# Thresholded attention and a SoLU feed-forward block on one core: the first four units' product with v taken in place, in 32-row tiles

## The chip, the core and the metric

The kernel runs on one core of a Trainium2 chip. The metric is the device time of one execution in microseconds (us). A core has a matrix engine (PE; its weight loads are listed apart as PEld), a vector engine (DVE), a scalar engine (ACT), a GpSimd engine (POOL), a queue engine that only issues transfers (SyncE, SP), and 16 DMA engines that all queues share. Each engine works through its own instructions in order and waits on semaphores where it needs another's result.

## The reference, cut to what matters

```python
# q, k, v: (8 batches, 8 heads, 576 positions, 64), float32; tau = 0.02
scores = (q @ k.T) / sqrt(64)
thresh = max(scores, axis=-1) - tau
scores = where(scores >= thresh, scores, -1e9)
attn = exp(scores - max(scores)); attn = attn / (sum(attn) + 1e-9)
x = attn @ v                          # then (batch, position, head * 64): 4608 x 512
h = x @ w_in                          # 512 -> 1024; the weights arrive as 64-bit floats
solu = h * softmax(h)
ln = (solu - mean) / sqrt(var + 1e-6) * g_ln
out = ln @ w_out                      # 1024 -> 512
```

## The kernel before

**Units and slots.** Heads go in pairs; a pair's two heads lie in the two 64-row halves of the tiles. A batch has four pairs. Its first 512 positions are cut into two kinds of 256 queries, its last 64 positions are kind 2. A unit is (batch, kind, pair); it has two slots r = 0 and 1 of 128 queries and two heads each. A batch has 18 slots, the program 144, one a round; some 17 rounds follow in which only the feed-forward block is left.

**One round** (the loop in the last 200 lines) writes each engine's instructions of that round, in an order set by hand (`tc.manual_schedule`): PE multiplies the slot's scores (`scores`, L480) into two PSUM tiles; DVE takes the row maxima (`maxes`, L502); ACT clips (`ramp`, L517) and takes the exponentials (`exps`, L526); a round later POOL normalises (`normalise`, L533 to L536) and DVE turns the weights in 32 x 32 blocks (`blocks`, L548) into the unit's tile T. PSUM has two tiles for the scores and two pairs of banks, `p0` and `p1`, for all else: the product with v takes one (`take("pv")`), a feed-forward tile's h one until it is multiplied, its output one.

**The product with v.** A block turn leaves each 32-key block of a query group on that group's own 32 partitions, so the keys do not lie where v has them. With slot r = 1, `blocks` therefore issues three transfers on SyncE's queue (L557 once, 576 KB; L559 twice, 288 KB each) that carry T into `wT`, where keys lie on 64 partitions as v's rows do. Some rounds later (`pv_due`) `attend_steps` multiplies: nine key chunks, two row halves, two heads, 36 products in tiles of 64 rows and 64 columns with 128 queries as the moving side (L590), each product two pairs of weight load and matmul. `attended` copies the result to xh on ACT (L622). The first four units, (0, 0, pair 0 to 3), are multiplied in rounds 5, 7, 9 and 10.

**The feed-forward block.** When a kind's four units are done, two tiles of 128 tokens are ready. A tile takes four quarter steps on PE, one a round: h in two halves (L655), and, after softmax, statistics, the exchange of halves by DMA (`ff_swap`, L737) and a block turn (`ff_turn`, L747), the product with w_out in two halves (L760). The first tile's h is multiplied in rounds 11 and 12. A line `if rnd == 13` lets the second tile's h follow before the first tile's product with w_out.

**The start.** Rounds 0 to 15 also decode one piece of the weights each (`weight_load` on SyncE's queue, L275; L286, L292, L306 and L309 on DVE; L291 on ACT; L319 on POOL). Pair 1, 2 and 3 of batch 0 are turned by PE in rounds 0, 2 and 4 with both bank pairs in use (`whole_pair`, L345). v is loaded by half batches: half 0 in rounds 0 and 1, half 1 in rounds 3 and 5 (L177, L182). Its columns hold four of each partition's positions; columns 4 to 7 hold those of the partition 64 away.

Of the kernel before, what the change touches and what calls it, by code (L numbers as in the profile page):

```python
# [8 lines left out]
F32 = mybir.dt.float32  # L9
# [7 lines left out]
P = 128  # L17
# [3 lines left out]
def kernel(  # L21
# [27 lines left out]
    nc = tc.nc  # L49
    B, H, S, D = q.shape  # L50
# [39 lines left out]
    NK = S // 64  # L90

    halves = {}
# [3 lines left out]
    units = {}  # L96
    xh = {}
# [3 lines left out]
    pairs_free = ["p0", "p1"]  # L101

    def take(name):
        tag = pairs_free.pop(0)
        return tag, ps_mm.tile([P, 1024], F32, tag=tag, name=name)
# [44 lines left out]
    def load_v(b, hf, parts=(0, 1, 2)):  # L150
        d = halves.setdefault((b, hf), {})
        hs = slice(4 * hf, 4 * hf + 4)

        if b > 1:
            if 0 in parts:
                d["v"] = loads.tile([P, 4, NK, D], F32, tag="v", bufs=3, name="v")
            to = d["v"].rearrange("p h m d -> p h (m d)")
            rows = v_rows[64 * (H * b + 4 * hf) :][0:256]
            for part in parts:
                nc.sync.dma_start(**(  # L160
                    dict(
                        out=to.rearrange("p (e o) n -> p o e n", o=2)[:, 0],
                        in_=rows.rearrange("(e r) n -> r e n", e=2),
                    ),
                    dict(out=to[:, 1], in_=rows[64:192]),
                    dict(out=to[ROWS[1], 3], in_=rows[0:64]),
                    dict(out=to[ROWS[0], 3], in_=rows[192:256]),
                )[part])
            return
        if 0 in parts:  # L170
            d["v"] = loads.tile([P, 4, NK, D], F32, tag="v", bufs=3, name="v")
        rest = v[b, hs, 0:SM, :].rearrange("h (p t) d -> p h (t d)", t=4)
        for part, to, rows, of in (
            (0, 0, slice(0, P), slice(0, P)), (1, 4, ROWS[0], ROWS[1]), (1, 4, ROWS[1], ROWS[0])
        ):
            if part in parts:
                nc.sync.dma_start(  # L177
                    out=d["v"][rows, :, to : to + 4].rearrange("p h t d -> p h (t d)"),
                    in_=rest[of],
                )  # L180
        for rows in ROWS if 2 in parts else ():
            nc.sync.dma_start(  # L182
                out=d["v"][rows, :, NK - 1], in_=v[b, hs, SM:S, :].rearrange("h p d -> p h d")
            )

    qk_rows = {
        nm: x.rearrange("b h (i a t) d -> a (b h i) (t d)", a=2, t=NK)
# [167 lines left out]
    def source(i):  # L355
        b, hp = divmod(i, NP)
        return halves[b, hp // 2], 2 * (hp % 2)
# [182 lines left out]
    def blocks(s):  # L540
        b, kind, hp, r = slots[s]
        key = (b, kind, hp)
        if r == 0:
            units[key] = dict(T=work.tile([P, NB, 2, 2, 32], F32, tag="T", name="T"))
        u = units[key]
        T = u["T"]
        for h, w in enumerate(live.pop(s)["w"]):
            nc.vector.transpose(out=T[:, :, r, h, :], in_=w)  # L548
        if r == 0:
            return  # L550


        T = T.rearrange("p (c m) r h x -> p c (m r h x)", c=2)
        u["wT"] = wT = work.tile([P, 2, NK, 2, 2, 32], F32, tag="wT", bufs=2, name="wT")
        to = wT.rearrange("p g m r h x -> p g (m r h x)")
        if kind < 2:
            nc.sync.dma_start(out=to[:, 1], in_=T[32:96])  # L557
            for half in range(2):
                nc.sync.dma_start(out=to[ROWS[half], 0], in_=T[96 * half : 96 * half + 32])  # L559
            return  # L560
        for g in range(2):
            for half in range(2):
                of = 64 * half + 32 * g
                nc.sync.dma_start(out=to[ROWS[half], g], in_=T[of : of + 32])  # L564

    def attend_steps(key):
        b, kind, hp = key
# [97 lines left out]
    def ff_max(t):  # L667
        d = ffn[t]
        d["nm"] = small.tile([P, 1], F32, tag="hm", name="hm")
        nc.vector.tensor_reduce(out=d["nm"], in_=d["h"], axis=AX.X, op=ALU.max, negate=True)  # L670

    def ff_exp(t):
        d = ffn[t]

        starts.append(t)
        tag = "xh1" if rnd > NS and len(starts) % 2 else "u"
        d["u"] = work.tile([P, DFF], F32, tag=tag, bufs=1, name="u")
        d["se"] = small.tile([P, 1], F32, tag="se", name="se")
        nc.scalar.activation(  # L679
            out=d["u"], in_=d["h"], func=AF.Exp, bias=d["nm"], scale=1.0, accum_out=d["se"]  # L680
        )

    def ff_mul(t):
        d = ffn[t]
        nc.vector.tensor_tensor(out=d["u"], in0=d["h"], in1=d["u"], op=ALU.mult)  # L685
        pairs_free.append(d["tag"])

    def ff_sum(t):
        se = ffn[t]["se"]
        nc.gpsimd.tensor_scalar(out=se, in0=se, scalar1=1e-9, scalar2=None, op0=ALU.add)  # L690
        nc.gpsimd.tensor_tensor(out=se, in0=se, in1=mone[:, 0:1], op=ALU.pow)
# [110 lines left out]
    PER = NS // B  # L802
    LAG_PV = 3

    pv_due = []
    for s, (b, kind, hp, r) in enumerate(slots):
        if r == 1:
            pv_due.append((s + LAG_PV + (s < 6 or s in (11, PER - 1, PER + 9)), (b, kind, hp)))

    def first_slot(i):  # L810
        return PER * (i // NP) + 2 * (i % NP)
# [12 lines left out]
    load_at = {}  # L824
# [12 lines left out]
    for i in range(2 * NP, NPAIR, 2):  # L837
        b, hf = divmod(i // 2, 2)
# [3 lines left out]
        for nm, pieces_at in zip("qk", ats):  # L842
            for a, at in enumerate(pieces_at):
                at += PER * b
                if b == 2:
                    of = at - 3 - (at in (PER + 7, PER + 9))
                else:
                    of = (at - 3) // 4 * 4
# [19 lines left out]
    with tc.manual_schedule():  # L868
# [14 lines left out]

        pieces = {r: x for x, r in enumerate(range(16))}
        whole = {0: 1, 2: 2, 4: 3}
        for r, hf, parts in ((0, 0, (0,)), (1, 0, (1, 2)), (3, 1, (0,)), (5, 1, (1, 2))):
            load_at[r] = [lambda hf=hf, parts=parts: load_v(0, hf, parts)]

        ready = []
        rnd = 0  # L890
# [7 lines left out]
        while True:  # L898
# [10 lines left out]
            if rnd == NS:  # L909
# [6 lines left out]
                    cur = None  # L916
                    quarter = 0
                assert quarter != 3
            if rnd == 13:
                prev, cur, quarter = cur, None, 0  # L920
            if (
                cur is None and quarter == 0 and ready and ready[0][0] <= rnd
# [9 lines left out]
            if more:  # L932
# [3 lines left out]
                while preps and preps[0][0] <= rnd and preps[0][1] <= room:  # L936
                    _, n, make, _ = preps.pop(0)
# [27 lines left out]
                weight_c(pieces[rnd - 1])  # L965
            for job in middle.pop(rnd, []):
                job()
            due = bool(pv_due) and pv_due[0][0] <= rnd
            step = None
            if quarter < 2 and cur is not None:  # L970
# [17 lines left out]
            if step == ("h", 0):  # L988
                ff_h(cur, 0, rnd + 1 < NS, beside)
                quarter = 1  # L990
            elif step == ("h", 1):
                ff_h(cur, 1, None, beside)
                quarter = 2
                by = rnd + 2 * (rnd == 14)
                late.setdefault(by, []).append(lambda t=cur: (ff_max(t), ff_exp(t)))
                late.setdefault(by + 1, []).append(lambda t=cur: (ff_mul(t), ff_sum(t)))
                middle.setdefault(by + 2, []).append(lambda t=cur: ff_stats(t))
                if rnd + 6 < NS:
                    norms[by + 3] = cur
                else:  # L1000
                    late.setdefault(rnd + 2, []).append(lambda t=cur: ff_norm(t))
                middle.setdefault(by + 3, []).append(lambda t=cur: (ff_norm2(t), ff_swap(t)))

                at = by + 4 if more or not ready or len(ready[0][1][0]) == 1 else rnd + 6
                if cur == (0, 1, 1):
                    middle.setdefault(rnd + 6, []).append(lambda t=cur, at=rnd + 6: ff_turn(t, at))
                else:
                    late.setdefault(at, []).append(lambda t=cur, at=at: ff_turn(t, at))
                if not more:
                    between.append(cur)  # L1010
                    cur = None
                    quarter = 0
            elif step == ("o", 0):
                if prev is not None:
                    ff_o(prev, 0)
                quarter = 3
            elif step == ("o", 1):
                if prev is not None:
                    ff_o(prev, 1)
                    last = not (more or ready or cur or between)  # L1020
                    begin.setdefault(rnd + 1, []).append(lambda t=prev, last=last: ff_out(t, last))
                    late.setdefault(rnd + 1, []).append(lambda t=prev, last=last: ff_store(t, last))
                prev, cur = cur, None
                quarter = 0
            if attending is not None:
# [3 lines left out]
                b, kind, hp = attending  # L1029
# [16 lines left out]
            if rnd in pieces:  # L1046
                x = pieces[rnd]
# [45 lines left out]
```

## Time and profile before

| | |
|---|---|
| time, three runs | 861.92, 864.92, 865.21 us; median 864.92 |
| profiled execution | 869.02 us, its span 867.2 us |
| busy share of the span | PE 95%, weight loads 70%, DVE 79%, ACT 66%, POOL 58% |
| mean granted PE clock | 0.976 |
| DMA | 168.54 MB, mean 194 GB/s; data queue q1 76.3% of the 16 engines |
| chain that ended last | PE 79%, DMA 8%, DVE 4%, ACT 4% |

The page gives one profiled execution: busy times by engine, the span in 40 slices of 21.7 us (a digit is a busy share in tenths), the DMA queues, the chain of work that ended last followed back from the end, and the groups of instructions that cost most. A row of the timeline gives start, duration, engine, line, operation, output and input, and in brackets the idle time before it and what ended it. A busy PE is not one at its peak, since matmuls overlap.

### The profile page before, as it was taken

The page shows a single profiled execution, that of the slowest core. Times are in us where ns is not written, and L with a number is a line of the kernel's source. Part 1 is how long each engine was busy: PE and PEld are TensorE (multiplying, and loading weights), DVE is VectorE, ACT ScalarE, POOL GpSimd, SP SyncE. Part 2 cuts the span into 40 slices and gives each one's busy share as a digit, 9 for nine tenths or more (in the row PEclk, how much of TensorE's full clock was granted, in tenths as well). Part 3 has the DMA queues.
Part 4 walks back from the last instruction along what each step waited for, and adds up shares of the span by engine and source line. Part 5 has one row for each costly group of instructions (what it writes and reads, how often), then busy time and mean ns, then how long its engine had stood idle before and what let it go on. Part 6 is the DMA issues. An engine that isn't in the chain of part 4 may idle for free.

```text
span 867.2 us, 36122 instructions
## 1 busy us (share of the span) xinstructions
PE 822.9 (95%) x15361; PEld 605.8 (70%) x15361; DVE 681.7 (79%) x1248; ACT 573.6 (66%) x1153; POOL 500.2 (58%) x938
## 2 busy tenths in 40 slices
PE   5668799989999999999999999999999999999997
PEld 3446466667677776899777766777777777777655
DVE  4988878878788888888888887888788887787361
ACT  5877876667677767777666766777677776776121
POOL 2886656556756666565656665565666655555120
PEclk9769999999999999999999999999999999999999
DMA  8999887998888878898888787888788787655312
GB/s 256 252 251 227 191 210 181 210 236 210 215 206 226 208 183 214 208 221 203 196 207 225 207 187 185 217 220 207 183 230 229 197 192 180 163 136 139 69 38 62
DMA packets 83712, 168.54 MB, mean 194 GB/s; under 512 B 15448, under 2 KB 45152, under 8 KB 83552
## 3 DMA queue, kind: packets, MB, share of 16 engines
q1 hardware_dynamic: 82416, 164.25, 76.3%
q8 instruction: 120, 1.97, 1.0%
q10 hardware_dynamic: 1136, 2.00, 0.7%
q14 instruction: 40, 0.33, 0.1%
HBM read 46.14 MB, written 9.44 MB: 64 GB/s over the span
## 4 chain that ended last, share of the span: by engine, by line
PE 79%; DMA 8%; DVE 4%; ACT 4%; SPq 2%; issue 2%; POOL 1%; ACTq 0%; DVEq 0%
PE o_ps L760 26%; PE h_ps L655 20%; PE pv L590 14%; PE s_ps L480 14%; DMA wT<-T 6%; PE h_ps L645 3%; ACT w L517 1%; DVE w L502 1%; ACT w L526 1%; DVE T L548 1%; DMA q<-in_q_dram 1%; DMA qT<-flip 1%; SPq L564 1%; DMA k<-in_k_dram 1%; SPq L559 0%
## 5 line engine op out<-in xcount | busy, mean ns | idle before, releaser
L760 PE MATMUL o_ps<-w,uT 64*64 64x256 f32 x4608 | 271.6, 378 | 1.2 <-ACT xe L622 0.6
L502 DVE CUSTOM_DVE_ANT_0 w<-s_ps,tau_t 128x576 f32<-128x576 f32 x280 | 200.0, 751 | 90.0 <-PE s_ps L480 61.6
L517 ACT ACTIVATE w<-s_ps,nth 128x576 f32<-128x576 f32 x280 | 196.9, 739 | 107.0 <-DVE nth L502 89.6
L760 PEld LDWEIGHTS o_ps<-w,uT 64*64 64x64 f32 x4608 | 212.7, 134 | 66.1 <-ACT xh L622 12.1
L536 POOL TENSOR_SCALAR w<-w,sm 128x576 f32<-128x576 f32 x288 | 222.1, 783 | 14.3
L548 DVE STREAM_TRANSPOSE T<-w 128x576 f32<-128x576 f32 x288 | 207.6, 755 | 20.6 <-POOL w L536 19.1
L655 PE MATMUL h_ps<-w,xh 64*64 64x512 f32 x1856 | 221.0, 589 | 0.1
L526 ACT ACTIVATE w<-w,ntau 128x576 f32<-128x576 f32 x288 | 219.7, 767 | 0.0
L590 PEld LDWEIGHTS pv<-wT,v 64*64 64x64 f32 x5760 | 175.2, 138 | 45.4 <-issue 24.5
L480 PE MATMUL s_ps<-kT,qT 64*64 64x64 f32 (+1 forms) x2048 | 177.1, 422 | 13.3 <-ACT w L517 10.9
L590 PE MATMUL pv<-wT,v 64*64 64x128 f32 (+1 forms) x5760 | 178.0, 266 | 10.9 <-DMA wT<-T 7.8
L655 PEld LDWEIGHTS h_ps<-w,xh 64*64 64x64 f32 x1856 | 118.0, 133 | 78.8 <-issue 45.7
L533 POOL TENSOR_SCALAR sm<-sm 128x2 f32<-128x2 f32 x144 | 37.0, 257 | 201.8 <-ACT w L526 198.5
L534 POOL TENSOR_TENSOR sm<-sm,mone 128x2 f32<-128x2 f32 x144 | 108.7, 755 | 12.0
L480 PEld LDWEIGHTS s_ps<-kT,qT 64*64 64x64 f32 x2048 | 73.0, 139 | 21.7 <-ACT w L517 15.7
L622 ACT COPY xh<-pv 128x256 f32<-128x256 f32 x64 | 25.1, 393 | 82.4 <-PE pv L590 82.4
L721 ACT ACTIVATE V<-u,nb,rs 128x1024 f32<-128x1024 f32 x36 | 44.7, 1241 | 39.3 <-POOL nb L711 32.4
L747 DVE STREAM_TRANSPOSE uT<-V 128x1024 f32<-128x1024 f32 x36 | 44.2, 1227 | 18.1 <-DMA V<-u 17.7
L526 ACT ACTIVATION_READ_ACCUMULATOR w<-w,ntau 128x1 f32 x288 | 55.6, 193 | 0.0
L685 DVE TENSOR_TENSOR u<-h_ps,u 128x1024 f32<-128x1024 f32 x36 | 42.8, 1190 | 9.8 <-ACT u L679 9.8
L726 DVE TENSOR_SCALAR u<-u,rs,nb 128x1024 f32<-128x1024 f32 x36 | 35.3, 982 | 17.6 <-ACT V L721 17.6
L670 DVE TENSOR_REDUCE hm<-h_ps 128x1 f32<-128x1024 f32 x36 | 42.9, 1192 | 4.8 <-PE h_ps L645 2.7
(90 smaller groups left out, 568.1 us busy)
## 6 DMA issues: line engine op xcount, KB each, us to landing
wT<-T SPq DMA_DIRECT2D x160, 288.0 KB, 6.7
wT<-T SPq DMA_DIRECT2D x64, 576.0 KB, 5.4
V<-u SPq DMA_DIRECT2D x144, 64.0 KB, 3.3
out_dram<-ob SPq DMA_DIRECT2D x71, 128.0 KB, 2.5
q<-in_q_dram SPq DMA_DIRECT2D x24, 288.0 KB, 5.7
qT<-flip SPq DMA_DIRECT2D x48, 144.0 KB, 4.2
k<-in_k_dram SPq DMA_DIRECT2D x24, 288.0 KB, 6.1
kT<-flip SPq DMA_DIRECT2D x48, 144.0 KB, 3.9
```

Source lines behind the costliest of these rows:

```text
L480: nc.tensor.matmul(out=ps[h][ROWS[y], ks], lhsT=lhsT, rhs=d["kT"][ROWS[h], ks], start=True, stop=True,)
L502: nc.vector.tensor_tensor_reduce(out=w, in0=ps[:, 0:S], in1=(zero if loose else tau_t).to_broadcast([P, S]), scale=1.0, scalar=BIG, op0=AL ...
L517: nc.scalar.activation(out=d["w"][x], in_=d["w"][x] if d["loose"] else d["ps"][x][:, 0:S], func=AF.Prelu, bias=d["nth"][x], scale=-1.0, al ...
L526: nc.scalar.activation(out=w, in_=w, func=AF.Exp, bias=ntau, scale=1.0, accum_out=sm[:, x : x + 1])
L534: nc.gpsimd.tensor_tensor(out=sm, in0=sm, in1=mone, op=ALU.pow)
L536: nc.gpsimd.tensor_scalar(out=w, in0=w, scalar1=sm[:, x : x + 1], scalar2=1.0, op0=ALU.mult, op1=ALU.mult)
L548: nc.vector.transpose(out=T[:, :, r, h, :], in_=w)
L590: nc.tensor.matmul(out=to, lhsT=d["v"][ROWS[u], (h0 + h - u) % 4 if b > 1 else h0 + h, m ^ 4 * u if m < 8 and b < 2 else m,], rhs=rhs, sta ...
L655: mm = nc.tensor.matmul(out=h[ROWS[y], f], lhsT=x[ROWS[r], c, ROWS[y]], rhs=w1_parts[ROWS[r], c, part ^ r], start=part == 0 and c == 0, st ...
L721: nc.scalar.activation(out=V, in_=u, func=AF.Identity, bias=nb, scale=rs)
L747: nc.vector.transpose(out=uT, in_=d["V"].rearrange("p y (m x) -> p m y x", x=32))
L760: nc.tensor.matmul(out=d["o"][ROWS[z], 512 * (r ^ other) : 512 * (r ^ other) + 256], lhsT=d["uT"][ROWS[r], m].rearrange("p y x -> p (y x)" ...
```

## The change

The first four units are multiplied straight out of T. Their block transfers are gone. `blocks` reads the weights of these units in another order, pairs of keys 288 columns apart side by side, so that each 32-key block holds 32 neighbouring rows of v. A block then meets v in tiles of 32 rows and 64 columns: for each of the 18 blocks, the four query groups and the two heads there is one product with 64 queries as the moving side. The rows of v must lie on the query group's own partitions; v itself has two of the four row groups there, and a second copy `v2`, moved on by 32 partitions by two DMAs (864 and 288 KB) for each half of batch 0, has the other two. The four groups are summed in four PSUM banks, so a unit takes both bank pairs, and ACT copies the result in two pieces. The units are multiplied in rounds 5, 6, half of the third in 7 and 8 each, and 9. The first feed-forward tile starts in round 10 for 11, the second one round earlier too. Half 1 of v is loaded in rounds 2 and 3 for 3 and 5; the copies are issued at the ends of rounds 3 and 5. The third unit's T and the second copy lie in the tiles of `wT`, which has no other use until round 10.

```diff
+    FIRST = 4
+    def turn_v(b, hf):
+        d = halves[b, hf]
+        tag = ("v", "wT")[hf]
+        d["v2"] = v2 = loads_or_work(tag)
+        nc.sync.dma_start(out=v2[32:P], in_=d["v"][0:96])
+        nc.sync.dma_start(out=v2[0:32], in_=d["v"][96:P])
...
         if r == 0:
-            units[key] = dict(T=work.tile([P, NB, 2, 2, 32], F32, tag="T", name="T"))
+            tag = "wT" if s == 4 else "T"
+            units[key] = dict(T=work.tile([P, NB, 2, 2, 32], F32, tag=tag, bufs=2, name="T"))
...
         for h, w in enumerate(live.pop(s)["w"]):
+            if b == kind == 0:
+                w = w.rearrange("p (c j k) -> p j k c", c=2, k=16)
             nc.vector.transpose(out=T[:, :, r, h, :], in_=w)
-        if r == 0:
+        if r == 0 or b == kind == 0:
             return
...
+    def attend_in_place(key):
+        b, kind, hp = key
+        unit = units[key]
+        T = unit["T"]
+        unit["y"] = take("pv"), take("pv")
+        d, h0 = source(b * NP + hp)
+        for j in range(NB):
+            m, c = divmod(j, 2)
+            for a in range(4):
+                group = slice(32 * a, 32 * a + 32)
+                y = unit["y"][a // 2][1].rearrange("p (u n) -> p u n", u=2)[:, (a ^ a >> 1) & 1]
+                nm, of = ("v", a) if (c ^ a) & 1 == 0 else ("v2", (a - 1) % 4)
+                col = m if m == 8 else m % 4 + 4 * (of != c + 2 * (m // 4))
+                for h in range(2):
+                    nc.tensor.matmul(
+                        out=y[ROWS[h], 0:64].rearrange("p (r x) -> p r x", r=2),
+                        lhsT=d[nm][group, h0 + h, col],
+                        rhs=T[group, j, :, h],
+                        start=j == 0, stop=j == NB - 1,
+                    )
+                    yield
+    def attended_in_place(key):
...
+        for half, (tag, y) in enumerate(units.pop(key)["y"]):
+            nc.scalar.copy(...)
+            pairs_free.append(tag)
...
-        if r == 1:
-            pv_due.append((s + LAG_PV + (s < 6 or s in (11, PER - 1, PER + 9)), (b, kind, hp)))
+        if r == 1 and s >= 2 * FIRST:
+            pv_due.append((s + LAG_PV + (s in (11, PER - 1, PER + 9)), (b, kind, hp)))
+    in_place = {5: ((0, 4),), 6: ((1, 4),), 7: ((2, 2),), 8: ((2, 2),), 9: ((3, 4),)}
...
-        for r, hf, parts in ((0, 0, (0,)), (1, 0, (1, 2)), (3, 1, (0,)), (5, 1, (1, 2))):
+        for r, hf, parts in ((0, 0, (0,)), (1, 0, (1, 2)), (2, 1, (0,)), (3, 1, (1, 2))):
             load_at[r] = [lambda hf=hf, parts=parts: load_v(0, hf, parts)]
+        for r, hf in ((3, 0), (5, 1)):
+            load_at.setdefault(r, []).append(lambda hf=hf: turn_v(0, hf))
...
-            if rnd == 13:
+            if rnd == 12:
                 prev, cur, quarter = cur, None, 0
...
+            for hp, parts in in_place.get(rnd, ()):
+                key = (0, 0, hp)
+                steps = units[key].setdefault("steps", attend_in_place(key))
+                for _ in zip(range(NB * 8 * parts // 4), steps):
+                    pass
...
+                    attended_in_place(key)
+                    if hp == NP - 1:
+                        ready.append((rnd + 1, [(0, 0, 0), (0, 0, 1)]))
...
-                by = rnd + 2 * (rnd == 14)
+                by = rnd + 2 * (rnd == 13)
```

More of the change, by code (lines that the diff above doesn't have):

```diff
@@ L184, in load_v, with loads_or_work @@
             )
+    FIRST = 4
[5 more added lines that the diff above has]
+        nc.sync.dma_start(out=v2[0:32], in_=d["v"][96:P])
+    def loads_or_work(tag):
+        if tag == "v":
+            return loads.tile([P, 4, NK, D], F32, tag="v", bufs=3, name="v2")
+        return work.tile([P, 4, NK, D], F32, tag="wT", bufs=2, name="v2")
     qk_rows = {
@@ L564, in blocks @@
                 nc.sync.dma_start(out=to[ROWS[half], g], in_=T[of : of + 32])
+    def attend_in_place(key):
[20 more added lines that the diff above has]
+    def attended_in_place(key):
+        b, kind, hp = key
+        if hp == 0:
+            xh[b, kind] = work.tile([P, NP, 256], F32, tag="xh0", bufs=1, name="xh")
+        for half, (tag, y) in enumerate(units.pop(key)["y"]):
+            nc.scalar.copy(
+                out=xh[b, kind][:, hp].rearrange("p (r v u x) -> p v u r x", r=2, v=2, u=2)[:, half],
+                in_=y.rearrange("p (u n) -> p u n", u=2)[:, :, 0:64].rearrange(
+                    "p u (r x) -> p u r x", r=2
+                ),
+            )
+            pairs_free.append(tag)
     def attend_steps(key):
@@ L967 @@
                 job()
+            for hp, parts in in_place.get(rnd, ()):
[3 more added lines that the diff above has]
+                    pass
+                units[key]["parts"] = units[key].get("parts", 0) + parts
+                if units[key]["parts"] == 4:
+                    assert next(steps, None) is None
+                    attended_in_place(key)
+                    if hp == NP - 1:
+                        ready.append((rnd + 1, [(0, 0, 0), (0, 0, 1)]))
             due = bool(pv_due) and pv_due[0][0] <= rnd
```

## The prediction

> **What bounds the kernel now.** I read the page, then the chain of waits of the first 130 us, then the timelines of DVE, PE and SyncE there. Outside rounds 2 to 20 both kernels put the same instructions in the same order: following the round loop's rules for both, the first product with w2 falls into round 17 in either, and from round 21 on every step is the same. So only the first 130 us can change; the rest is a constant shift, however full PE is there.
>
> The page (q8: packets, MB, share of the engines): PE is full from the fifth slice on, but not before, where the 16 DMA engines are busiest. PE's instructions come in by q8: 120 packets of 16 KB for 2 x 15361 matmuls and weight loads, so 256 of them to a packet.
>
> ```profile
> PE 822.9 (95%) x15361; PEld 605.8 (70%) x15361; DVE 681.7 (79%) x1248; ACT 573.6 (66%) x1153; POOL 500.2 (58%) x938
> PE   5668799989999999999999999999999999999997
> DMA  8999887998888878898888787888788787655312
> q8 instruction: 120, 1.97, 1.0%
> ```
>
> The chain of waits: near 55 us it leaves DVE for a block transfer, and PE's product with v stands 12 us behind that.
>
> ```profile
> 53.84 0.74 DVE T L548
> 54.63 0.58 SPq L557
> 55.26 0.60 SPq L559
> 55.92 12.04 DMA wT<-T
> 68.00 3.53 PE pv L590 x65
> 72.66 3.46 PE h_ps L655 x32
> ```
>
> DVE's timeline, first row-maximum of rounds 5, 6, 9, 10 and 11 (last bracket: idle before, and who ended it). Rounds 5 to 9 follow each other by (56.48 - 36.69) / 4 = 4.95 us with DVE full: two maxima, two transposes, 2.2 us of weight decoding. Then scores(10) and scores(11) stand on PE behind products that wait for their transfers.
>
> ```profile
> 36.69 0.74 DVE L502 CUSTOM_DVE_ANT_0 w<-s_ps,tau_t 128x576 f32<-128x576 f32 x1
> 41.60 0.76 DVE L502 CUSTOM_DVE_ANT_0 w<-s_ps,tau_t 128x576 f32<-128x576 f32 x1 [0.15 <-PE s_ps L480]
> 56.48 0.74 DVE L502 CUSTOM_DVE_ANT_0 w<-s_ps,tau_t 128x576 f32<-128x576 f32 x1
> 64.61 0.76 DVE L502 CUSTOM_DVE_ANT_0 w<-s_ps,tau_t 128x576 f32<-128x576 f32 x1 [2.21 <-PE s_ps L480]
> 72.50 0.76 DVE L502 CUSTOM_DVE_ANT_0 w<-s_ps,tau_t 128x576 f32<-128x576 f32 x1 [3.25 <-PE s_ps L480]
> ```
>
> PE's timeline: pairs (weight load and matmul) of 64 columns at half clock and at full clock, of 128 columns at full clock, and a stall for which nothing else is waited.
>
> ```profile
> 31.79 1.05 PE L345 MATMUL tp<-ident,k 64*64 64x64 f32 x28
> 134.71 1.26 PE L590 MATMUL pv<-wT,v 64*64 64x64 f32 x70
> 80.13 2.23 PE L590 MATMUL pv<-wT,v 64*64 64x128 f32 x70
> 95.77 0.26 PE L345 MATMUL s_ps<-ident,k 64*64 64x64 f32 x1 [1.61 <-issue]
> ```
>
> **What goes.** Twelve block DMAs (4 units of 1152 KB) and the two waits above: 1.21 us (DVE, before 59.12) + 2.21 + 3.25 = 6.7 us of DVE idle time. The half feed-forward steps move one round forward (round 10 for 11), which shifts DVE work between rounds 10 and 19 but adds none.
>
> **What comes on PE.** A unit has 18 x 4 x 2 = 144 products, two pairs each as now (the page's 5760 for 2880 products): 288 pairs for 72. No row shows 32-row tiles. Nearest: 64 columns in four tiles, (1.26 - 0.21) / 70 = 15 ns a pair at full clock, (1.05 - 0.32) / 28 = 26 ns at half clock. Eight tiles could halve that; nothing shows that they do, nor a gain below it, so 7.5 and 26 ns are the ends and I take 15: 288 x 15 = 4.3 us a unit (2.2 to 7.5) against 72 x 28 = 2.0 us. The Trainium skill ("TensorE: Matmul & The Clock Gate", the section on why the gap is 56 ns) holds that matmul starts are never closer than about 25 ns. By that rule a unit takes 7.2 us; the trace disagrees with its 15 ns.
>
> **PE's instruction supply.** A unit is 576 instructions, 2.25 packets. Set against the count of PE's instructions, q8's packets show a store of two blocks: packet k starts only when block k + 1 has been entered, 1.0 us after at the earliest, usually 2 to 4 us after while DMA is full; it takes 0.9 to 1.6 us; and in the two stalls named "issue" (1.6 and 1.4 us), both on a multiple of 256 instructions, PE goes on 1.25 and 1.47 us after the packet's end. So a block costs at least 1.2 + 1.0 + 1.3 = 3.5 us: 27 ns a pair, when PE runs through more than it holds. Now it never does: its densest 512 instructions take 8.0 us. A whole-unit round has 608 instructions (16 pairs are the scores), 2.4 blocks: 8.3 us, less what lies ready at its start; a half-unit round 1.25 blocks, 4.4 us, under DVE's 4.95.
>
> **The copy v2.** SyncE issues half 0's copy at the end of round 3, behind that round's weight load (raw, 29.5 to 31.4 us now) and four DMAs of v, which took 3.1 us (41.18 to 44.3): issue at about 34.5 us. It waits for v, which has long landed. Landing: 5.4 us (576 KB over the whole run) to 10.5 us (up to 80 us): 40 to 45 us. Little else is queued, since unit 0's and 1's transfers are gone: I take 40.5. Unit 0's first product with v2 is its third, so PE stands from 36.7 to 40.5, with scores(6) behind it. Half 1's copy, issued near 41.5, is needed near 57 and hidden.
>
> **What costs nothing.** DVE's transposes read w in pairs 1152 bytes apart; the nearest row, reading every second element, takes 746 ns for 755 (L213 against L548). ACT has two smaller copies a unit for one: 4 x 0.3 us, beside PE. Queue: they wait for PE's unit, with the next round's decode step (L291) behind them, which DVE needs only after two maxima and two transposes (2.9 us). If that cover failed, it would cost up to 0.7 us a round. v2's third buffer of "v" is free again when batch 1's v is loaded.
>
> **The sum, round by round** (first maximum; now in brackets). Unit 0: 40.5, half clock, 438 instructions at hand, the last 138 at full clock: ends 47.2; scores, round 6: 48.3 (41.6). Unit 1: 86 instructions left, blocks at 49.2 and 52.6: ends 54.4; the scores behind it cross into a block that comes at 56: round 7: 56.3 (46.6). Half units: DVE's pace, round 8: 61.3 (51.8), round 9: 66.2 (56.5). Unit 3: starts 64.9, blocks at 66.2 and 69.6, ends 71.1; round 10: 72.0 (64.6). Feed-forward steps, 3.4 us each on PE: round 11: 76.8 (72.5). From there DVE's own work: round 11 waits for h and takes 7.3, then 6.2, 6.6, 6.2, 6.5, about 4.7, 5 and 5 to round 19: 47.5, where now it is 121.7 - 72.5 = 49.2. Plus the turn of the second tile, 1.2 us, which leaves round 20. Shift: 4.3 - 1.7 - 1.2 = +1.4. Two things are missing in that: the stalls that the ideal rounds 11 to 19 leave out (now 1.7 in round 14, about 2 each in 17 and 18; I give back 2), and block delays above the least while the copies fill DMA, half the 2 us between least and usual, for two blocks: 2. Together about +5 us.
>
> The profiled execution took 869.0 us (span 867.2, 1.8 around it), 4.1 over the median of 864.9. The shift is a difference inside the trace: 874 on that run, 870 on the median.
>
> **Rivals.**
> A, instructions arrive in time and PE is no bound. For it: 118 of 120 blocks passed without a stall. Then unit 0 ends near 44 to 46.6 and DVE paces rounds at 4.95: round 11 at 69.5 to 72.5, end -1.5 to -5, so 860 to 863.5, say 862. The Trainium skill ("Runtime: NRT & Kernel Launch", Instruction fetch mechanics) says that crossing a 16 KiB boundary is mostly hidden and gives PE room for 2048 instructions. By that rule it is this case; the trace shows two blocks.
> B, blocks come as late as the packet at 93.09, 6.3 us after its block was passed. That is 6 to 7 us a block; it decides as soon as the copies and loads keep DMA full past 45 us. Four blocks 3 us later: +12, 877.
> C, the copy lands by 37: unit 0 starts as now and about 4 us return: 866. Against it: the issue at 34.5.
>
> **Chances.** Forecast 0.50 (own range 866 to 875), A 0.27, B 0.13, C 0.10. Under 0.5%, 4.3 us, a measurement of this kernel hardly tells from no change. Slower: 0.36 of the forecast, all of B, 0.01 of C: 0.50. Faster: 0.14, A's lower half. Same: 0.14 of the forecast, 0.13 of A, 0.09 of C: 0.36. Range 860 to 878: A's lower end, and B beyond the forecast.
>
> **What would show it.** Right: PE pv stalls "<-issue" inside units 0, 1 and 3, q8 packets 3 to 5 us apart there; first v2 product near 40.5; round 10's maximum at 70 to 74 and round 20's 3 to 7 us later than now. Wrong: units of under 4.5 us without gaps (A), or DVE full from round 6 on.

## The result and the profile after

The changed kernel takes 885.43 us (median of 4 runs, 883.87 to 886.79), the kernel before 864.09 us (4 runs, 861.92 to 865.21). The ratio is 1.0249, its 95% interval 1.0218 to 1.0281: 21 us slower, where 5 were forecast and the range ended at 878. The profiled execution took 886.79 us, span 885.0. It lies 1.4 us over its median, that of before 4.9 over the median of its four runs (4.1 over that of the three known at the prediction), so the two traces differ by 17.8 us where the medians differ by 21.3.

The page of the changed kernel. In slices 2 to 4 (22 to 88 us) PE's busy digits stand at 3, 6 and 7 where before had 6, 6 and 8, and DMA's in slices 3 and 4 at 3 and 3 for 9 and 9: PE has more instructions and yet is idle more, and DMA is not what is short behind 50 us. The 864 matmuls more (16225 for 15361) and their weight loads are seven packets more on q8, the queue that brings PE's instructions.

```profile
PE 825.2 (93%) x16225; PEld 587.9 (66%) x16225; DVE 681.3 (77%) x1248; ACT 574.5 (65%) x1157; POOL 499.7 (56%) x938
PE   4367879999999999999999999999899999999997
DMA  8933979799889878888788878888778887655312
q8 instruction: 127, 2.08, 1.0%
```

DVE's timeline shows the first row maximum of rounds 6, 7, 10 and 11 (before: 41.60, 46.58, 64.61, 72.50). The shift is there at once: +16.3 in round 6, +19.9 in round 7; then it falls to +17.7 in round 11, and is +17.6 at the last slot of the program.

```profile
57.90 0.76 DVE L516 CUSTOM_DVE_ANT_0 w<-s_ps,tau_t 128x576 f32<-128x576 f32 x1 [16.50 <-PE s_ps L494]
...
66.47 0.76 DVE L516 CUSTOM_DVE_ANT_0 w<-s_ps,tau_t 128x576 f32<-128x576 f32 x1 [3.90 <-PE s_ps L494]
...
83.83 0.76 DVE L516 CUSTOM_DVE_ANT_0 w<-s_ps,tau_t 128x576 f32<-128x576 f32 x1 [1.84 <-PE s_ps L494]
...
90.23 0.76 DVE L516 CUSTOM_DVE_ANT_0 w<-s_ps,tau_t 128x576 f32<-128x576 f32 x1 [1.76 <-PE s_ps L494]
```

The chain of waits of the changed kernel, from the copy on. Up to 72 us it is half 0's copy of v, 11.37 us from issue, then PE alone, with stops named "issue": time in which PE waits for nothing that the profile shows.

```profile
34.54 11.37 DMA v<-v
...
45.96 3.28 PE pv L599 x172
49.23 5.10 issue
54.34 1.41 PE pv L599 x66
55.74 2.13 PE s_ps L494 x16
57.87 2.42 PE pv L599 x131
60.29 1.58 issue
```

PE's timeline gives the same stops for the first two units (288 pairs of weight load and matmul each) and the fourth, with the idle time in brackets.

```profile
44.88 0.60 PE L599 MATMUL pv<-T,v 32*64 32x64 f32 x12 [7.84 <-DMA v<-v]
45.96 3.28 PE L599 MATMUL pv<-T,v 32*64 32x64 f32 x203 [0.48 <-DMA v<-v]
54.34 1.41 PE L599 MATMUL pv<-T,v 32*64 32x64 f32 x69 [5.10 <-issue]
...
57.80 2.49 PE L599 MATMUL pv<-T,v 32*64 32x64 f32 x171
61.87 1.80 PE L599 MATMUL pv<-T,v 32*64 32x64 f32 x117 [1.58 <-issue]
...
69.88 2.20 PE L494 MATMUL s_ps<-kT,qT 64*64 64x64 f32 x16
...
76.04 2.31 PE L599 MATMUL pv<-T,v 32*64 32x64 f32 x185 [0.47 <-ACT xh L612]
81.35 1.31 PE L599 MATMUL pv<-T,v 32*64 32x64 f32 x103 [3.00 <-issue]
```

All stops named "issue" here lie a multiple of 256 instructions apart, if the few semaphore instructions between them are counted. PE goes on at 54.34, 61.87, 81.35 and 86.43; a q8 packet ended at 52.91, 60.44, 80.03 and 85.14, that is 1.3 to 1.4 us earlier each time. From 51 to 88 us ten packets came, and the data queue q1 was mostly idle (21.5% of the engines' time):

```profile
q1 hardware_dynamic: 759, 2.46, 21.5%
q8 instruction: 10, 0.16, 1.9%
```

Their starts are 3.67, 3.70, 3.74, 3.70, 3.73, 3.76, 4.95, 4.84 and 3.67 us apart. So a block of 256 instructions takes 3.7 us here even with little traffic beside it, and at two places 4.9; PE stops where it gets through a block in less.

The theory to be tested is that one part of the 21 us is the supply of instructions, by their number, and the rest the copies of v: half 0's, for which PE waits, and half 1's, behind which a packet stands.

### The profile page after: what moved, and what is told of

It reads as the page before. It is cut to its first block, busy times and chain, and to the rows that moved or that the text cites. A ratio compares the mean times of both kernels' runs of the same rounds, so it can differ in the third digit from the quotient of the medians.

```text
span 885.0 us, 37833 instructions
## 1 busy us (share of the span) xinstructions
PE 825.2 (93%) x16225; PEld 587.9 (66%) x16225; DVE 681.3 (77%) x1248; ACT 574.5 (65%) x1157; POOL 499.7 (56%) x938
## 4 chain that ended last, share of the span: by engine, by line
PE 86%; ACT 4%; issue 3%; DVE 3%; DMA 3%; SPq 0%; POOL 0%; ACTq 0%; DVEq 0%
PE o_ps L812 27%; PE h_ps L707 23%; PE s_ps L494 16%; PE pv L642 14%; PE h_ps L697 3%; PE pv L599 2%; ACT w L531 1%; DMA v<-v 1%; ACT w L540 1%; DMA wT<-T 1%; DVE w L516 1%; DMA k<-in_k_dram 1%; DVE T L565 0%; DVE w L320 0%; PE s_ps L359 0%
## 5 line engine op out<-in xcount | busy, mean ns | idle before, releaser
L812 PE MATMUL o_ps<-w,uT 64*64 64x256 f32 x4608 | 266.8, 376 | 1.2 <-issue 0.6
L812 PEld LDWEIGHTS o_ps<-w,uT 64*64 64x64 f32 x4608 | 217.4, 133 | 60.0 <-issue 12.1
L707 PE MATMUL h_ps<-w,xh 64*64 64x512 f32 x1856 | 218.7, 591 | 1.4 <-issue 1.4
L642 PEld LDWEIGHTS pv<-wT,v 64*64 64x64 f32 x5472 | 155.0, 134 | 40.6 <-issue 26.8
L494 PE MATMUL s_ps<-kT,qT 64*64 64x64 f32 (+1 forms) x2048 | 172.9, 425 | 9.4 <-ACT w L531 8.4
L707 PEld LDWEIGHTS h_ps<-w,xh 64*64 64x64 f32 x1856 | 102.3, 134 | 96.4 <-issue 77.9
L642 PE MATMUL pv<-wT,v 64*64 64x128 f32 (+1 forms) x5472 | 157.7, 260 | 6.6 <-issue 4.3
L494 PEld LDWEIGHTS s_ps<-kT,qT 64*64 64x64 f32 x2048 | 66.6, 139 | 18.3 <-ACT w L531 11.8
L778 DVE TENSOR_SCALAR u<-u,rs,nb 128x1024 f32<-128x1024 f32 x36 | 35.0, 971 | 17.5 <-ACT V L773 17.4
```

The lines of the kernel that those rows point to most:

```text
L494: nc.tensor.matmul(out=ps[h][ROWS[y], ks], lhsT=lhsT, rhs=d["kT"][ROWS[h], ks], start=True, stop=True,)
L642: nc.tensor.matmul(out=to, lhsT=d["v"][ROWS[u], (h0 + h - u) % 4 if b > 1 else h0 + h, m ^ 4 * u if m < 8 and b < 2 else m,], rhs=rhs, sta ...
L707: mm = nc.tensor.matmul(out=h[ROWS[y], f], lhsT=x[ROWS[r], c, ROWS[y]], rhs=w1_parts[ROWS[r], c, part ^ r], start=part == 0 and c == 0, st ...
L812: nc.tensor.matmul(out=d["o"][ROWS[z], 512 * (r ^ other) : 512 * (r ^ other) + 256], lhsT=d["uT"][ROWS[r], m].rearrange("p y x -> p (y x)" ...
```

## The experiments

Times are medians beside the kernel before on the same chip; e1 to e4 have only two executions each. A round is called late or early by its first row maximum against the profiled run of before, which was 4.9 us over its median; where in it those lie is not known.

### The copies

**No copies** (e1): the DMAs of `turn_v` are gone, and the products read `v` in place of the copy.

```diff
-        for r, hf in ((3, 0), (5, 1)):
-            load_at.setdefault(r, []).append(lambda hf=hf: turn_v(0, hf))
...
-                        lhsT=d[nm][group, h0 + h, col],
+                        lhsT=d["v"][group, h0 + h, col],
```

> The changed kernel without the four DMAs of v2: the products that read v2 read v's own rows on the same partitions instead, so their part of the sum is another one; count and shape of all PE instructions are as in the changed kernel. Theory (the copy lands late, and PE's instruction blocks of 256 come late, above all behind the copies): unit 0 starts at 36.7 us and goes on without the 8.3 us of waiting; gaps named issue remain in units 0, 1 and 3 but each under 2.5 us, and their packets start within 2 us of the time they are due; round 6's first maximum near 47 (57.9 in the changed kernel), round 10's near 70, time 870 to 874. Rival (products in 32-row tiles are slow by themselves, or PE pays for changing tile shapes): unit 0 takes as long from its start as it does in the changed kernel without its two waits, but rounds 6 to 10 still take 26 us, and the time is 876 to 878, only the 8.3 us of waiting less.

Measured: 876.89 us for 866.37, ratio 1.0126 (1.0060 to 1.0193). Round 6 comes at 44.95, yet round 10 is still 9.1 us late. PE stops 2.50, 2.15, 1.94, 0.43 and 3.01 us for "issue" in units 0 to 3. The stops are the theory's, their size is not: 10 us in sum, and the time falls into the rival's range.

**One copy** (e4): half 1's copy is gone; units 2 and 3 read half 0's.

```diff
         d = halves[b, hf]
+        if hf:
+            d["v2"] = halves[b, 0]["v2"]
+            return
```

> The changed kernel without half 1's copy: units 2 and 3 read half 0's copy in its place, so their result is another one. Theory (the 5.1 us gap in unit 0 is an instruction packet that stands behind half 1's copy in the DMA engines): the gap after the first 430 instructions of unit 0 falls under 2.5 us, its packet starts within 2 us of being due, round 6's maximum near 54.5 (57.9), time 881 to 883. Rival (the packet is late because PE stood still for the copy before, or for a reason that has nothing to do with DMA load): the gap stays above 4 us and the time within 1.5 us of the changed kernel.

Measured: 881.69 us, ratio 1.0182 (1.0120 to 1.0244). PE's timeline, to be set beside that of the changed kernel: the wait for half 0's copy is the same, the stop in unit 0 is 1.35 us for 5.10.

```profile
45.77 3.35 PE L602 MATMUL pv<-T,v 32*64 32x64 f32 x203 [0.57 <-DMA v<-v]
50.47 1.41 PE L602 MATMUL pv<-T,v 32*64 32x64 f32 x69 [1.35 <-issue]
```

The packet that ends this stop starts at 47.85 here and at 51.82 with half 1's copy in the queues, PE being 0.2 us earlier. Nothing else was taken away, so that copy held the packet for 3.8 us.

**Copy early** (e2): half 0's copy is issued a round sooner, half 1 of v loaded a round later.

```diff
-        for r, hf, parts in (... (2, 1, (0,)), (3, 1, (1, 2))):
+        for r, hf, parts in (... (3, 1, (0,)), (4, 1, (1, 2))):
-        for r, hf in ((3, 0), (5, 1)):
+        for r, hf in ((2, 0), (5, 1)):
```

> The changed kernel with half 0's copy issued at the end of round 2 instead of 3, ahead of half 1's loads, which go to rounds 3 and 4. Theory: the copy is issued as soon as v has landed, near 29 us, lands at 36 to 38, and the wait of 7.8 us in unit 0 shrinks to under 1.5; block 5 of PE's instructions is then due near 40, while half 1's v and its copy fill DMA, so a gap of 3 to 5 us named issue stays in unit 0; round 6's maximum 50 to 53 (57.9), time 877 to 881. Rival (the copy's time is set by DMA's total load, not by its place in the queue): it still lands after 43, round 6 above 56, time over 883.

Measured: 877.47 us, ratio 1.0133 (1.0045 to 1.0221). The wait for v is gone; the stops named "issue" in the units are 2.33, 0.16, 4.34, 0.73, 0.60 and 2.70 us, 10.9 in sum. The long stop came in unit 1 and not in unit 0, so round 6, at 45.88, was earlier than expected. With all data there, the time is that of no copies at all.

### The number of instructions without the rest

**Same count, same tile** (e3): the kernel before, each product of the first four units cut into four of 32 queries, one behind the other.

```diff
+                        if b == kind == 0:
+                            parts = [(to[:, g, r], rhs[:, g, r]) for g in range(2) for r in range(2)]
```

> The kernel before, block transfers and 64-row tiles as they were, but each of the 36 products of the first four units is cut into four of 32 queries: 144 products, 576 PE instructions a unit, as many as in the changed kernel, at the rounds of the kernel before. Theory (instruction supply): gaps named issue of 1 to 4 us appear inside units 0 to 3, at multiples of 256 instructions, and the time is 4 to 10 us over the kernel before: 868 to 874. Rival (it is the 32-row tiles, the copies and the order, not the count): 288 pairs at 15 ns are 4.3 us a unit for 2 to 3.9, no such gaps, the time within 3 us of the kernel before.

Measured: 909.59 us, ratio 1.0504 (1.0379 to 1.0629), with only 4.4 us of "issue" stops in the run and none in the four units. It tells nothing of the count: with four products in a row on one tile a pair takes 15.85 us / 285 = 56 ns (granted clock 0.53), and 128 pairs, a block, take 7.1 us, so PE is slower than its packets.

```profile
36.86 15.85 PE L598 MATMUL pv<-wT,v 64*64 64x32 f32 x285 [1.53 <-ACT qe L423]
```

**Same count, tiles in turn** (e5): the same cut, the four parts as the outer loop, so that successive products go to different tiles.

```diff
-                for u in range(2):
+                for x, u in [(x, u) for x in (range(4) if b == kind == 0 else [None]) for u in range(2)]:
```

> The kernel before, with its transfers, rounds and queues, but the 36 products of each of the first four units are cut into four of 32 queries each, in tiles of 64 rows, ordered so that successive products go to different tiles: 144 products, 576 instructions a unit as in the change, no copy of v, no 32-row tile. Theory (PE's instruction supply): in at least three of the four units PE stops at a multiple of 256 instructions for 1 to 4 us, named issue, and goes on 1.2 to 1.6 us after the end of a q8 packet; round 10's first row maximum 4 to 8 us later than before, time 4 to 10 us over the kernel before. Rival (the cost lies in the 32-row tiles, the copies or the new rounds, not in the count): no such stop, the units take 144 x 2 x 13 to 15 ns = about 4 us where they had 3.5 and end behind DVE's other work, time within 3 us of the kernel before.

Measured: 887.54 us for 864.22, ratio 1.0249 (1.0212 to 1.0286). Every unit now stops once for "issue": 1.42, 1.83, 2.00 and 1.34 us, on multiples of 256, 1.3 to 1.6 us behind a packet's end. So neither 32-row tiles nor copies are needed for the stops. The size was missed by far (+23 us for 4 to 10): the third row of the timeline below is 28 ns a pair at half clock, where I had 13 to 15. The granted clock was 0.5 from 36 to 70 us here, although the first stop came only at 43. How much of the 23 us is count and how much pace, this kernel leaves open.

```profile
36.85 6.18 PE L592 MATMUL pv<-wT,v 64*64 64x32 f32 x219 [1.80 <-ACT qe L423]
44.45 2.03 PE L592 MATMUL pv<-wT,v 64*64 64x32 f32 x67 [1.42 <-issue]
...
52.52 7.83 PE L592 MATMUL pv<-wT,v 64*64 64x32 f32 x283
62.18 0.32 PE L592 MATMUL pv<-wT,v 64*64 64x32 f32 x3 [1.83 <-issue]
```

### Half the instructions

**Half the key blocks** (e6): there are no copies, and only every second key block is multiplied.

```diff
-        for j in range(NB):
+        for j in range(0, NB, 2):
```

> The change without the copies of v (its products read v where they would read the copy, so the wrong rows of v), and with every second key block only: 72 products, 288 instructions a unit, half of the sum left out. Everything else as in the run without copies, which was 10.5 us over the kernel before. Theory (instruction supply): a round now takes 352 instructions, 1.4 blocks, which a block every 3.5 us covers in 4.8 us, under DVE's 4.95; the gaps named issue in units 0 to 3 shrink to under 1 us each, round 10's first maximum falls from 73.7 us to 62 to 65, time 860 to 867. Rival (the order of steps or the rounds of the feed-forward block cost the 10 us, not the instructions): round 10's maximum stays over 70 us and the time over 872.

Measured: 862.74 us for 864.22, ratio 0.9982 (0.9957 to 1.0007). Round 10 comes at 61.70. That is as the theory has it, but this kernel halves PE's work too.

**Two heads a product, no copies** (e9): all key blocks are multiplied with half the instructions, and each does more work.

```diff
-                for h in range(2):
-                    nc.tensor.matmul(out=y[ROWS[h], 0:64]..., lhsT=d["v"][group, h0 + h, col], rhs=T[group, j, :, h], ...)
+                nc.tensor.matmul(out=y[:, 0:128], lhsT=(columns of h0 and h0 + 1 side by side), rhs=T[group, j] as (r h x), ...)
...
+            for h in range(2):
+                nc.scalar.copy(out=xh[b, kind][ROWS[h], hp]..., in_=y[ROWS[h]]...[:, :, :, h])
```

> The run without copies (its products read v where they would read the copy, so the wrong rows of v; 876.9 us), but the two heads of a product taken together: v's columns of both heads as 128 stationary columns, 128 queries as the moving side, the two halves that belong together are copied out. 72 products, 288 instructions a unit for 576, with no key block left out; a pair now takes 128 columns in four tiles, 28 ns at full clock and 55 ns at half by the rows of 128 columns, so PE's own work grows: 144 x 28 = 4.0 us a unit (7.9 at half clock) for 3.3. v of batch 0 is stored with its columns ordered position, head, and loaded in pieces of 256 bytes. Theory (the number of instructions is the cost): gaps named issue in units 0 to 3 under 2 us in sum, DVE's idle time between 36 and 76 us 4 us or less where the run without copies had 13, round 10's first maximum at 62 to 67 us, time 862 to 868. Rival (PE's work in these rounds is the cost, and halving it made the half-block run fast): round 10 over 70 us, time over 872.

Measured: 864.97 us for 864.59, ratio 1.0008 (0.9975 to 1.0042). PE's timeline has no stop named "issue" in the four units. One window from 36 to 76 us, in the columns PE, weight loads, DVE, ACT, POOL busy (with counts), granted PE clock, DMA share, GB/s; first the changed kernel, then no copies, then two heads:

```profile
36.00:76.00 40.00, 23.85 (x928) 15.78 (x928) 18.73 (x41) 16.14 (x38) 15.74 (x20) 0.66 0.49 121
```
```profile
36.00:76.00 40.00, 29.10 (x1248) 19.48 (x1252) 26.57 (x58) 23.24 (x52) 23.68 (x29) 0.79 0.31 93
```
```profile
36.00:76.00 40.00, 36.48 (x788) 23.63 (x788) 38.00 (x79) 35.65 (x80) 32.32 (x41) 1.00 0.58 151
```

With 288 instructions a unit PE is busier (36.5 us for 29.1), and DVE is nearly full (38.0 for 26.6). PE's work was not the bound; the count was. The granted clock is 1.00 for 0.79 in this window too, so part of what was won is PE's pace, and how much of that the stops had cost is not shown. This decides against e9's rival and takes the doubt from e6. One thing did not carry through: round 11 comes 4.4 us earlier than before, the last slot 0.5.

**Two heads, with the copies** (e10): e2 with the products of e9.

> The run of the early copy (877.5 us, nothing left out) with the two heads of a product taken together as in the other kernel of this call: 288 instructions a unit. Theory: the early copy is there before unit 0, half 1's copy ends near 56 us and is needed near 57, packets still come late while DMA is full up to 55 us: gaps of 2 to 4 us in units 0 and 1 instead of 8.7; round 10's maximum at 64 to 69 us, time 863 to 870. If the copies alone were the cost (rival), it stays within 3 us of 877.

Measured: 873.62 us, ratio 1.0100 (1.0062 to 1.0137), above the theory's 870. Units 0 and 1 pass without a stop; unit 2 stands 5.05 us for half 1's copy, which landed at 52.6. I had compared that landing with the wrong round: the unit's first half is due in round 7, at 47.5.

**The third unit a round later** (e12): this is e10 with the whole of unit 2 in round 8.

```diff
-    in_place = {5: ((0, 4),), 6: ((1, 4),), 7: ((2, 2),), 8: ((2, 2),), 9: ((3, 4),)}
+    in_place = {5: ((0, 4),), 6: ((1, 4),), 8: ((2, 4),), 9: ((3, 4),)}
```

> The early copies with two heads a product (873.6 us), but the third unit whole in round 8 instead of half in round 7 and half in round 8, the fourth in round 9. In the run before, its third unit stood 5.05 us for half 1's copy, which landed at 52.6 us; now it is asked for at about 52. Nothing is left out. Theory (instruction count and copies are the whole loss): no wait of over 1.5 us for v, no gap named issue over 1 us in units 0 to 3, round 8's maximum within 1.5 us of the kernel before, round 10 at 62 to 65 us; time within 3 us of the two-heads run without copies, which was level with the kernel before: 862 to 868. Rival (the copies cost otherwise, by the DMA time they take from packets and loads): round 10 at 67 us or later, time 870 to 875.

Measured: 870.38 us for 863.75, ratio 1.0048 (1.0021 to 1.0076): the rival's numbers, with round 10 at 67.97, and the theory's 862 to 868 missed. What the trace shows is not the rival's packets, though: no stop for instructions in the units, and round 8 only 0.80 us late; but the copy, issued at 47.94 for 44.02 in e2, lands at 54.1 and 55.1 (its two DMAs), and what follows runs at half clock (granted 0.5 from 52.8 to 59.7):

```profile
51.40 0.48 PE L609 MATMUL pv<-T,v 32*128 32x128 f32 x2
54.14 0.81 PE L609 MATMUL pv<-T,v 32*128 32x128 f32 x6 [2.26 <-DMA v<-v]
55.12 6.22 PE L609 MATMUL pv<-T,v 32*128 32x128 f32 x136 [0.17 <-DMA v<-v]
62.40 4.40 PE L609 MATMUL pv<-T,v 32*128 32x128 f32 x144
```

136 pairs take 6.22 us, 144 of unit 3 at full clock 4.40. So behind a stop of 2.4 us some 2 us more were lost to the pace. No version with copies came out below the kernel before.

### Less of it, and more thinly

**Spread** (e7): this is e2 with each unit over two rounds, 5 to 12, and the first feed-forward step two rounds later.

```diff
-    in_place = {5: ((0, 4),), 6: ((1, 4),), 7: ((2, 2),), 8: ((2, 2),), 9: ((3, 4),)}
+    in_place = {r: (((r - 5) // 2, 2),) for r in range(5, 13)}
```

> The change with both copies of v issued early (the run of the early copy, 877.5 us) and each unit's 576 instructions spread over two rounds, rounds 5 to 12, the first feed-forward step in round 13 for 11. Nothing is left out. Theory: 288 instructions and 32 of the scores a round are 1.25 blocks, 4.4 us at 3.5 us a block, so the gaps named issue in these rounds nearly vanish (under 2 us in sum where the early copy alone had 10.7) and rounds 6 to 12 follow DVE's pace, round 10's maximum at 62 to 65 us; the feed-forward steps come two rounds later and cost some of that, time 864 to 872. Rival (a block crossing stalls PE whatever its density): gaps of 2 us or more stay at most multiples of 256, time 876 or more.

Measured: 888.45 us for 864.22, ratio 1.0273 (1.0235 to 1.0312). The theory's number fell: 11.7 us of stops stay (4.26, 0.24, 1.44, 0.30, 0.82, 1.81, 2.83). From 42.62 to 85.97 us the packets come 43.35 / 9 = 4.8 us apart, not 3.5; 320 instructions a round are 1.25 blocks, 6.0 us, and DVE's round is 4.95. The packets that end the two longest stops start while DMA is full (shares of 1.14 from 40 to 44 us and 1.09 from 77.5 to 81.5). The time is the rival's, though only two of the seven stops last 2 us or more. And the time is lost later than either had it: round 11 comes at 72.19, level with the kernel before, and the lateness is 8.5 us at round 20, 16.7 at round 27 and 20.1 at the last slot. The feed-forward steps are later here; that part is not taken apart.

**The last two units only** (e8): units 0 and 1 go by transfers as before, 2 and 3 in place in rounds 8 to 10 with half 1's copy. **And with two heads a product** (e11): the same two units, in rounds 9 and 10.

```diff
-    in_place = {5: ((0, 4),), 6: ((1, 4),), 7: ((2, 2),), 8: ((2, 2),), 9: ((3, 4),)}
+    in_place = {8: ((2, 4),), 9: ((3, 2),), 10: ((3, 2),)}
...
+    in_place = {9: ((2, 4),), 10: ((3, 4),)}
```

> Half of the change: units 0 and 1 by block transfers as before (rounds 5 and 7), units 2 and 3 in place, unit 2 in round 8, unit 3 in halves in rounds 9 and 10; only half 1 of v is copied, issued in round 5. The feed-forward steps from round 11 as before. Nothing is left out. Theory: the two transfers whose waits stood before rounds 10 and 11 (2.21 and 3.25 us of DVE's idle time) are gone, the half units fit a block every 3.5 us, and the copy has over 10 us to land before unit 2: round 8 within 1.5 us of the kernel before, round 11's maximum at 69 to 73 us where it had 72.5, time 861 to 866, 0 to 4 us below the kernel before. Rival (instruction blocks of 2 us or more of delay remain in units 2 and 3, or the copy stands in the way of a packet): round 11's maximum at 74 us or later, time 867 to 875.

> The mixed kernel (873.3 us: units 0 and 1 by transfer, 2 and 3 in place, half 1's copy landed at 57.7 us), with the two heads of a product taken together and units 2 and 3 in rounds 9 and 10. Nothing is left out. Theory: unit 2 waits for the copy until about 58 us, both units then take 4.0 to 7.9 us with under 2 us of gaps, round 10 at 64 to 67 us, round 11 at 69 to 73 where the kernel before has 72.5; time 861 to 867. Rival (the copy, not the instructions, made the mixed kernel slow): round 11 at 77 us or later, time 870 to 875.

Measured: 873.29 us, ratio 1.0097 (1.0069 to 1.0125), and 874.75 us, ratio 1.0099 (1.0065 to 1.0133). Both missed the theory's time. In e8 the copy, issued at 42.5 behind two units' transfers, let unit 2 get going only at 57.7, and stops of 2.14 and 1.74 us follow; round 11 at 78.8, as the rival had it. In e11 the stops are gone and round 11 comes at 72.81, inside the theory's 69 to 73, level with the kernel before; yet the time is the rival's. Its last slot is only 3.1 us late in the traces, but its profiled execution (872.75) lies 2.0 us under its median and that of before 4.9 over, so these two profiles cannot tell where the 10 us between the medians lie. That stays open.

## Why the prediction was wrong, step by step

By the ratios, 2.5% is made up as follows: half 1's copy 0.7% (1.0249 to 1.0182), half 0's 0.6% (1.0182 to 1.0126), the number of instructions 1.2% (1.0126 to 1.0008), and 0.1% is left. The single steps have intervals of about 0.7% or more: by the times alone only the last is clear of noise, and the first two rest on the traces of e4 and e2.

- **Mechanism.** Right: PE's instruction supply takes the place of the transfers' waits. e9 halves the count, and what e1 without copies had kept of the loss goes with it.
- **Half 0's copy: the first step that failed.** I took the landing at 40.5 out of 40 to 45; PE had all of it at 45.96, which is +5.5 us in round 6. The bet was that little else is queued; DMA's share stayed at about 1.0 until 50 us, with loads of v, weights and both copies. The bracket's 5.4 us is a row of 576 KB transfers and its 10.5 us one of 288 KB; the copy's two DMAs, of 864 and 288 KB, took 11.0 and 11.4 us from issue until PE went on. The latest landing of that bracket was nearly right.
- **Half 1's copy, "hidden": the second.** Its data were in time. But it was looked at only as something that PE waits for, and a packet of 16 KB stood behind it. Unit 0's row of the sum has no stop at all, and the 2 us for late blocks at its end were all that stood for this; the stop took 5.10 us, and e4 gives 3.75 of it back. The two make 10.6 us; less 1.0, the products being quicker, that is round 6's miss (57.90 for 48.3).
- **A block at 3.5 us.** Nearly right: it was 3.7 us. Rounds 6 to 7, 7 to 8 and 8 to 9 took 8.57, 5.64 and 4.60 us for 8.0, 5 and 4.9.
- **Unit 3 and the first feed-forward steps.** Two packets came 4.95 and 4.84 us apart; the stops of 3.00 and 1.37 us made rounds 10 and 11 2.9 us longer than forecast. In sum round 11 was 13.4 us later than in the prediction.
- **A pair at 15 ns.** It lay between the ends that I had named: (2.31 - 0.21) / 185 = 11.4 ns at full clock, (3.28 - 0.32) / 203 = 14.6 ns at half. The Trainium skill ("TensorE: Matmul & The Clock Gate", the section on why the gap is 56 ns) has no starts below 25 ns; these rows disagree, more than the prediction's did.
- **Behind round 11.** Forecast +0.7 us to the end, found -0.1, but that is luck: the shift falls from 17.7 to 12.6 us and rises again. That the rest is one constant shift was wrong: from round 25 on it wanders between 12.5 and 17.6 us. At 637 us, in a stage that both kernels share, there is a stop of 2.4 us that before does not have, and across it (rounds 111 to 113) the shift grows by 4.2 us:

```profile
639.90 0.36 PE L642 MATMUL pv<-wT,v 64*64 64x64 f32 x1 [2.43 <-issue]
```

All seven profiled kernels with 16225 matmuls (e1 to e5, e7 and this one) stop there, for 2.2 to 2.7 us, and lose 2.6 to 4.8 us; none of the seven with fewer does. So more instructions also move the places where a block ends, and a block that ends in a dense stage costs there. Of the 9.0 us by which e1's last slot is late, 4.6 arise at this stop: by these traces, about half of what the number of instructions costs is not lost in the first four units.

- **The rivals.** A, instructions in time, came true only where the count was halved; e9's 865 is 3 us over its 862. B's condition, DMA full past 45 us, came true, for one block and not four. C was wrong. The Trainium skill ("Runtime: NRT & Kernel Launch", Instruction fetch mechanics) says that crossings are mostly hidden. That held in the first rounds of the kernel before and of e9, where a stage takes about one block in 4 to 5 us; in units 0, 1 and 3 of the changed kernel, which take more, a block costs 3.7 us or more. The same section gives PE room for 2048 instructions and, further down, only two lines of 16 KiB; the packets here fit the two.

Of the signs named, stops inside units 0, 1 and 3 and packets 3 to 5 us apart came; the first product with v2 (44.88 for 40.5), round 10 (83.83 for 70 to 74) and round 20 (+17.5 for 3 to 7) did not.

## What to carry to other kernels

Count PE's instructions by stage, not only its columns: here 256 of them cost 3.7 to 4.9 us, so small tiles pay only while a stage needs less than one such block in that time, and doubling the stationary columns to halve the count was worth 1.2% although PE then worked longer. A change of the count also moves every block's end behind it, and part of that 1.2% was lost so: look for new stops in stages that the change does not touch. Before a bulk copy is called hidden, look at everything that shares the DMA engines with it, the packets with the instructions too. Where a landing time is bracketed and DMA is full in the trace, take the late end.

## What the runs showed of the hardware

- In the 14 kernels profiled (before, after and twelve experiments), no two of PE's packets (some 120 to 127 in each) start less than 3.36 us apart, though most take 0.9 to 1.7 us themselves; the closest two of each kernel lie 3.36 to 3.67 us apart.
- A stop can be followed by a slower clock. In the changed kernel the granted clock was 0.5 from about 39 to 49, 52 to 59 and 63 to 73 us, with PE busy in most of the last stretch; the scores took 2.20 us there for 1.21 at 82.59 us. In e9, without stops, it was 1.00 from 36 to 76 us. Stops are not the only cause: in e5 it was 0.5 well before the first stop. The Trainium skill ("TensorE: Matmul & The Clock Gate", Part 1) gives half speed after an idle window of about 3.4 us and full speed after a busy one; the drop at 52 us, behind the stop of 5.10 us, agrees; the one at 63 us, behind a stop of only 1.58, and the nine mostly busy microseconds at half speed that follow do not.
- Products in a row on one tile took 56 ns a pair with 32 queries (e3, granted clock 0.53); the same products over four tiles in turn took 28 ns at half clock (e5).
